# Loading two chunks of k ahead of the filter and moving four tap units into the wait for it, in a long-convolution (H3) layer with an MLP

## The chip, the cores and the metric

The kernel runs on one core of a Trainium2 chip. The metric is the device time of one execution in microseconds (us). Engines are named as the profile names them: PE is TensorE's matmuls, PEld its weight loads, DVE is VectorE, ACT is ScalarE, POOL is GpSimd, SP is SyncE, which issues the loads of k, v and ssm_k.

## The reference, cut to what matters

```python
k_shift = sum over t of k_pad[:, t:t+S, :] * shift_k[:, 3-t]     # 4 taps along the sequence
kv   = k_shift * v
kv_f = rfft2(kv padded to 2S);  kf_f = rfft2(ssm_k padded to 2S)
y    = irfft2(kv_f * kf_f)[:S] + kv * ssm_D
h    = x + layernorm(x) * y                                     # x = q
out  = h + relu(layernorm(h) @ w1) @ w2                         # the MLP, later in the kernel
```

S is 2048 and D is 512, in bfloat16. Two sequences are transformed: the filter ssm_k, and kv, the product of the shifted k with v. The change touches only the way there: loads, taps, the product with v, and the first stage of the filter's transform.

## The kernel before: the parts concerned

A *tap unit* is four matmuls that shift and scale one piece of k (128 channels by 512 tokens) into one PSUM buffer; there are 16 units, and units 4c to 4c+3 need chunk c of k and of v. After each unit VectorE multiplies the PSUM buffer with v into `kvx`. A *group* is the first stage of the filter's transform for an eighth of its columns: 64 pairs of a weight load and a small matmul. All PSUM tiles here come from one pool of eight buffers. In the code, letters such as `"DDDDADDA"` name the engine that copies out of PSUM: A is ScalarE, D is VectorE. A load *lands* when its last byte is in place.

```python
psum = pl.push("psF", bufs=8, space=PSUM)
...
# order of the loads on one queue; k and v are transposed by the DMA
for c, src in ((0, "k"), (0, "s"), (0, "v"), (1, "k"), (1, "v"), (2, "k"), (2, "v"), (3, "k"), (3, "v")):
    ...
table(cs, tsn)                    # sine table: two ScalarE operations
...
table(cc, r2[:], (0,))            # first half of the cosine table
...
def taps(u):
    c, rg = divmod(u, DC)
    ps = psum.tile([P, CH], F32, tag="ps", name="pkv")
    for j in range(KS):
        nc.tensor.matmul(out=ps[:], lhsT=wdiag[:, rg, j, :],
                         rhs=kT[:, rg, CH * c + 16 - j:CH * c + CH + 16 - j], ...)
    return u, ps

def times_v(u, ps):               # VectorE: kvx <- ps * v
    ...
first = [taps(u) for u in range(4)]
for q in range(8):                # 8 batches of 8 transposes of ssm_k, each copied out of PSUM
    to_rows(lambda n: skv[:, :, :, n], q, kfl, "DDDDADDA"[q])
    if q == 1:
        for u, ps in first:
            times_v(u, ps)
table(cc, r2[:], (1,))            # second half of the cosine table
...
for gb in range(8):
    for u in ((4, 5), (6,), (7, 8), (9,), (10, 11), (12,), (13, 14), (15,))[gb]:
        times_v(*taps(u))
    group_k(gb)                   # 64 pairs on TensorE, then four copies by ScalarE or VectorE
...
for q in range(8):                # 64 transposes of kvx: the yardstick "kvx start" below
    to_rows(lambda n: kvc[:, n // 4, :, n % 4], q, xfl, "DDADDADD"[q])
```

## Time and profile before

| | |
|---|---|
| median of 3 runs | 221.08 us (220.58 to 221.51) |
| span of the profiled run, granted clock | 218.7 us, 0.990 |
| transposes of ssm_k | 12.29 to 18.76 us |
| transposes of kvx begin ("kvx start") | 36.98 us |
| from kvx start to the end | 181.76 us |

The waits of the kernel before between 10 and 42 us (engine, line and tile, what it waited for, then us in all, times, longest) are:

```profile
PE pst L217 <- DMA pre<-in_A_ssm_k_dram: 2.1, 1, 2.1
PE ps L244 <- issue: 1.4, 2, 0.7
...
DVE kvx L278 <- DMA vT<-in_A_v_dram: 1.7, 2, 1.0
```

The first line is the wait that the change wants to fill. The second counts time in which TensorE waited for nothing that the profile shows.

### The profile page before, as it was taken

To read this page: it belongs to the slowest core of one execution; us is meant where nothing else is said; L and a number is where in the kernel's file an instruction comes from. 1 tells how busy PE (TensorE), PEld (TensorE's weight loads), DVE (VectorE), ACT (ScalarE), POOL (GpSimd) and SP (SyncE) were. 2 spreads that over 40 slices of the span, in tenths; PEclk is the share of its full clock that TensorE was granted. 3 is DMA by queue.
4 is the path that set the end of the run, shared out by engine and by line. 5 is a ranking of instruction groups with operands and counts; after the bars stand their busy time and mean duration, and the time that the engine had idled before them with its cause. 6 is when DMAs were issued, how large, how long until landed. Compare 5 with 4: busy or idle time off the path is not lost.

```text
span 218.7 us, 7281 instructions
## 1 busy us (share of the span) xinstructions
PE 202.8 (93%) x3103; PEld 139.4 (64%) x3122; DVE 148.2 (68%) x304; ACT 127.7 (58%) x242; POOL 65.9 (30%) x99
## 2 busy tenths in 40 slices
PE   7879889999979999989987899999999999999993
PEld 2276446999968999879965587444444444444442
DVE  7978868899979999957968779742973257130032
ACT  2587858788867888858966699003740066206500
POOL 6059920000029999969200120210021002000000
PEclk9969999999999999999999999999999999999999
DMA  6999960000000000059970000332022110421012
GB/s 96 383 224 191 142 136 7 3 4 3 6 3 0 1 0 3 1 134 216 305 252 3 6 0 3 42 77 55 24 52 63 42 47 0 96 57 42 0 42 54
DMA packets 30383, 15.40 MB, mean 70 GB/s; under 512 B 25520, under 2 KB 29072, under 8 KB 30224
## 3 DMA queue, kind: packets, MB, share of 16 engines
q1 hardware_dynamic: 29520, 14.76, 29.9%
q8 instruction: 24, 0.39, 0.8%
q10 hardware_dynamic: 832, 0.20, 0.4%
q14 instruction: 7, 0.06, 0.1%
HBM read 7.08 MB, written 2.10 MB: 42 GB/s over the span
## 4 chain that ended last, share of the span: by engine, by line
PE 83%; ACT 6%; DMA 4%; issue 2%; DVE 2%; SPq 1%; ACTq 0%
PE ps2m L568 17%; PE ps1m L556 16%; PE pz L482 8%; PE psi L449 7%; PE psy L375 7%; PE pst L217 5%; PE ps L244 4%; PE pkv L271 4%; PE ps2k L259 4%; DMA pre<-in_A_ssm_k_dram 4%; PE ps2k L261 3%; PE u L259 3%; PE u L261 3%; ACT ecore L143 1%; SPq L121 1%
## 5 line engine op out<-in xcount | busy, mean ns | idle before, releaser
L556 PE MATMUL ps1m<-hlnT,w 128*128 128x512 bf16 (+3 forms) x219 | 39.5, 336 | 0.3
L558 ACT ACTIVATE h1T<-ps1m 128x512 bf16<-128x512 f32 (+3 forms) x55 | 27.4, 514 | 21.2 <-PE ps1m L556 20.3
L568 PE MATMUL ps2m<-w,h1T 128*128 128x512 bf16 (+3 forms) x177 | 38.9, 366 | 0.7 <-issue 0.3
L570 DVE TENSOR_TENSOR o<-ps2m,xh 128x512 bf16<-128x512 f32 (+1 forms) x17 | 11.1, 659 | 38.1 <-PE ps2m L568 37.6
L556 PEld LDWEIGHTS <-w 128*128 128x128 bf16 (+1 forms) x220 | 21.7, 100 | 17.6 <-issue 1.4
L568 PEld LDWEIGHTS <-h1T 128*128 128x128 bf16 (+1 forms) x187 | 17.6, 98 | 21.2 <-issue 3.1
L365 DVE TENSOR_TENSOR t<-u,kf 128x704 fp32r<-128x704 f32 x32 | 26.7, 887 | 2.9 <-ACT usb L361 2.6
L365 POOL TENSOR_TENSOR t<-usb,kf 128x320 fp32r<-128x320 f32 x32 | 28.1, 922 | 1.4 <-ACT usb L361 1.0
L493 ACT CAST zt<-pz 128x512 bf16<-128x512 f32 x16 | 8.4, 592 | 29.2 <-PE pz L482 29.2
L482 PE MATMUL pz<-bp,ecore 32*32 32x128 f32 x1024 | 22.5, 384 | 2.3 <-issue 1.4
L231 ACT CAST a<-ps 128x512 fp32r<-128x512 f32 (+1 forms) x42 | 21.2, 575 | 4.3 <-PE ps L244 4.2
L502 POOL TENSOR_SCALAR rstd<-mv 128x4 f32<-128x4 f32 (+1 forms) x7 | 1.6, 232 | 70.3 <-DVE mv L509 70.3
L482 PEld LDWEIGHTS pz<-bp,ecore 32*32 32x32 f32 x1024 | 14.2, 103 | 9.4 <-issue 5.4
L231 ACT CAST kf<-psy 128x512 fp32r<-128x512 f32 x30 | 17.4, 640 | 1.7 <-PE psy L375 0.2
L233 DVE CAST a<-ps 128x512 fp32r<-128x512 f32 (+1 forms) x26 | 16.1, 647 | 3.1 <-PE ps L244 2.9
L507 DVE BATCH_NORM_STATS2 st<-xh 128x6 f32<-128x512 bf16 x28 | 17.4, 680 | 0.0
L449 PE MATMUL psi<-dre,kf 128*128 128x256 f32 x64 | 15.5, 284 | 0.9 <-ACT kf L231 0.9
L375 PE MATMUL psy<-t,ipos 128*128 128x512 f32 x48 | 15.8, 391 | 0.0
L271 PE MATMUL pkv<-kT,wdiag 128*128 128x512 bf16 x56 | 14.8, 380 | 0.8 <-DMA kT<-in_A_k_dram 0.3
L449 PE MATMUL psi<-dim,kf 128*128 128x256 f32 x64 | 15.4, 283 | 0.0
L209 POOL TENSOR_SCALAR c2n<-c2s 128x512 fp32r<-128x512 f32 x8 | 11.9, 1559 | 8.9 <-ACT c2s L177 8.9
L449 PEld LDWEIGHTS psi<-dre,kf 128*128 128x128 f32 x64 | 12.3, 192 | 1.3 <-ACT kf L231 1.3
(115 smaller groups left out, 377.0 us busy)
## 6 DMA issues: line engine op xcount, KB each, us to landing
pre<-in_A_ssm_k_dram SPq DMA_DIRECT2D x1, 2048.0 KB, 8.7
out_dram<-o SPq DMA_DIRECT2D x58, 32.0 KB, 1.6
xh<-in_A_q_dram SPq DMA_DIRECT2D x4, 384.0 KB, 6.8
w<-in_B_w_dram SPq DMA_DIRECT2D x1, 1376.0 KB, 12.7
w<-in_B_w_dram SPq DMA_DIRECT2D x1, 1280.0 KB, 15.8
xh<-in_A_q_dram SPq DMA_DIRECT2D x4, 128.0 KB, 2.8
hlnT<-hln SPq DMA_TRANSPOSE x12, 2.4
w<-in_B_w_dram SPq DMA_DIRECT2D x1, 96.0 KB, 15.4
```

The lines of the kernel that those rows point to most:

```text
L231: nc.scalar.copy(out=o, in_=i)
L233: nc.vector.tensor_copy(out=o, in_=i)
L259: nc.tensor.matmul(out=ps[:, kk, :], lhsT=w_re[:, k1, :], rhs=a_in(col(k1, 0)), start=True, stop=False, skip_group_check=True)
L271: nc.tensor.matmul(out=ps[:], lhsT=wdiag[:, rg, j, :], rhs=kT[:, rg, CH * c + 16 - j:CH * c + CH + 16 - j], start=(j == 0), stop=(j == KS ...
L365: eng.tensor_tensor(out=t[:, :, j, :], in0=in0.unsqueeze(1).to_broadcast([P, 2, n, 2]), in1=kfr[:, :, j, ks], op=ALU.mult)
L375: nc.tensor.matmul(out=psy[:], lhsT=m_[:], rhs=t_.rearrange("p j k -> p (j k)"), start=first, stop=not first)
L449: nc.tensor.matmul(out=ps[:, i, :], lhsT=kf[:, c, 4 * m:4 * m + 4, :].rearrange("p r k -> p (r k)"), rhs=d[:].rearrange("p a b -> p (a b)" ...
L482: nc.tensor.matmul(out=pz[32 * a:32 * a + 32, r4, l4, :], lhsT=ecore[rows, rho, n2, :], rhs=rhs, start=(rho == 0), stop=(rho == 1), tile_p ...
L507: nc.vector.bn_stats(out=st[:, t % 4, :], in_=xh[:, t, :])
L556: nc.tensor.matmul(out=ps1[:fsz, :], lhsT=w1[:, c, fc * P:fc * P + fsz], rhs=hlnTs[sc][:, c, part], start=(c == 0), stop=(c == DC - 1))
L558: nc.scalar.activation(out=h1s[sc][:fsz, fc, part], in_=ps1[:fsz, :], func=ACT.Relu)
L568: nc.tensor.matmul(out=ps2[:], lhsT=h1s[sc][:ksz, fc, i * P:(i + 1) * P], rhs=w2[:ksz, fc, ds], start=(fc == 0), stop=(fc == NFC - 1))
```

## The change

The intent is to give TensorE work while ssm_k is on its way. The second chunk of k is loaded ahead of ssm_k, so that eight tap units instead of four run before its transposes. Units 0 to 3 are copied out of PSUM by ScalarE and multiplied with v later on GpSimd, which reads that copy. Both halves of the cosine table come early, the groups get a new order of units, and the new letters give VectorE 12 of the groups' 32 copies instead of 8.

```diff
-    for c, src in ((0, "k"), (0, "s"), (0, "v"), (1, "k"), (1, "v"), (2, "k"), (2, "v"), (3, "k"), (3, "v")):
+    for c, src in ((0, "k"), (1, "k"), (0, "s"), (1, "v"), (0, "v"), (2, "k"), (2, "v"), (3, "k"), (3, "v")):
...
+    first = [taps(u) for u in range(8)]
+    ck = early.tile([P, DC, CH], F32, name="ck")
+    for u, ps in first[0:4]:
+        nc.scalar.copy(out=ck[:, u, :], in_=ps)
...
-    table(cc, r2[:], (0,))
+    table(cc, r2)
...
+        if h == 1:
+            for u in range(4):
+                times_v(u, ck[:, u, :], nc.gpsimd)
...
-        stage1(gb, kfl, ..., "AADAAADA")
+        stage1(gb, kfl, ..., "ADAADADA")
-    first = [taps(u) for u in range(4)]
...
-        to_rows(lambda n: skv[:, :, :, n], q, kfl, "DDDDADDA"[q])
+        to_rows(lambda n: skv[:, :, :, n], q, kfl, "DDDDDDAA"[q])
         if q == 1:
-            for u, ps in first:
+            for u, ps in first[4:8]:
                 times_v(u, ps)
-    table(cc, r2[:], (1,))
...
-        for u in ((4, 5), (6,), (7, 8), (9,), (10, 11), (12,), (13, 14), (15,))[gb]:
+        for u in ((8, 9), (10,), (11,), (), (12,), (13,), (14,), (15,))[gb]:
```

More of the change, by code (lines that the diff above doesn't have):

```diff
@@ L95 @@
     nc.sync.dma_start(out=wsh[:], in_=A_shift_k.rearrange("(r p) j -> p r j", p=P))
-    pre = slotA.tile([P, 4096 + 2048], I32, tag="A", name="pre")
+    pre = slotA.tile([P, 4096 + 2 * 2048], I32, tag="A", name="pre")
     skf = pre[:, 0:4096].bitcast(BF16)
@@ L159 @@
     nc.gpsimd.iota(r3[:], pattern=[[1, 64]], base=0, channel_multiplier=0)
-    r2 = early.tile([P, 32, 64], I32, name="w_r")
-    nc.gpsimd.iota(r2[:], pattern=[[2, 32], [128, 64]], base=1, channel_multiplier=0)
+    r2 = pre[:, 6144:8192].rearrange("p (k n) -> p k n", n=64)
+    nc.gpsimd.iota(r2, pattern=[[2, 32], [128, 64]], base=1, channel_multiplier=0)
     n1c = early.tile([P, 1], F32, name="n1c")
@@ L178, in table, with taps, times_v @@
                                  scale=hsc[:, dp:dp + 1], bias=hbi[:, dp:dp + 1])
+    kvx = early.tile([P, 16, DC, 32, 4], BF16, name="kvx")
+    def taps(u):
+        c, rg = divmod(u, DC)
+        ps = psum.tile([P, CH], F32, tag="ps", name="pkv")
+        for j in range(KS):
+            nc.tensor.matmul(out=ps[:], lhsT=wdiag[:, rg, j, :], rhs=kT[:, rg, CH * c + 16 - j:CH * c + CH + 16 - j],
+                             start=(j == 0), stop=(j == KS - 1))
+        return u, ps[:]
+    def times_v(u, ps, eng=nc.vector):
+        c, rg = divmod(u, DC)
+        split = "p (a h l) -> p a h l"
+        eng.tensor_tensor(out=kvx[:, :, rg, 8 * c:8 * c + 8, :].rearrange("p h a l -> p a h l"),
+                                in0=ps.rearrange(split, h=16, l=4),
+                                in1=vTs[c][:, rg, :].rearrange(split, h=16, l=4), op=ALU.mult)
     t1 = early.tile([P, 64], I32, name="f1_t")
@@ L192 @@
     _sin(dsc[:], t3[:], 64)
+    first = [taps(u) for u in range(8)]
+    ck = early.tile([P, DC, CH], F32, name="ck")
+    for u, ps in first[0:4]:
+        nc.scalar.copy(out=ck[:, u, :], in_=ps)
     tsn = pre[:, 4096:6144].rearrange("p (k n) -> p k n", n=64)
-    _turns(nc, tsn, r2[:], n2c[:], 8192, False)
+    _turns(nc, tsn, r2, n2c[:], 8192, False)
     table(cs, tsn)
@@ L201 @@
     nc.vector.tensor_copy(out=f1lo[:], in_=f1d[:])
-    _turns(nc, r2[:], r2[:], n2c[:], 8192, True)
-    table(cc, r2[:], (0,))
+    _turns(nc, r2, r2, n2c[:], 8192, True)
+    table(cc, r2)
     dtab = consts.tile([P, 8, DC, 8], BF16, name="dtab")
@@ L209 @@
         nc.gpsimd.tensor_single_scalar(out=cn[:, hs, :], in_=cs[:, hs, :].bitcast(F32), scalar=-1.0, op=ALU.mult)
-        if h == 0:
+        if h == 1:
+            for u in range(4):
+                times_v(u, ck[:, u, :], nc.gpsimd)
+        if h == 7:
             nc.gpsimd.tensor_copy(out=dtab[:], in_=d0[:].rearrange("p r (o g) -> p o r g", g=8))
@@ L262, in stage2 @@
                              skip_group_check=True)
-    kvx = early.tile([P, 16, DC, 32, 4], BF16, name="kvx")
-    def taps(u):
-        c, rg = divmod(u, DC)
-        ps = psum.tile([P, CH], F32, tag="ps", name="pkv")
-        for j in range(KS):
-            nc.tensor.matmul(out=ps[:], lhsT=wdiag[:, rg, j, :], rhs=kT[:, rg, CH * c + 16 - j:CH * c + CH + 16 - j],
-                             start=(j == 0), stop=(j == KS - 1))
-        return u, ps
-    def times_v(u, ps):
-        c, rg = divmod(u, DC)
-        split = "p (a h l) -> p a h l"
-        nc.vector.tensor_tensor(out=kvx[:, :, rg, 8 * c:8 * c + 8, :].rearrange("p h a l -> p a h l"),
-                                in0=ps[:].rearrange(split, h=16, l=4),
-                                in1=vTs[c][:, rg, :].rearrange(split, h=16, l=4), op=ALU.mult)
     def group_k(gb):
-        stage1(gb, kfl, lambda o, j, n: a1k[:, :, 32 * o + j:32 * o + j + n], "AADAAADA")
-    first = [taps(u) for u in range(4)]
+        stage1(gb, kfl, lambda o, j, n: a1k[:, :, 32 * o + j:32 * o + j + n], "ADAADADA")
     kfl = early.tile([P, 32, 2, 64, 2], BF16, name="kfl")
```

## The prediction

> **What bounds the kernel now.** I read the page first, then the chain that ended last in order of time, then busy time by stages, then the timelines of DVE, ACT, POOL and the DMA queue. The page's engine shares of the chain:
>
> ```profile
> PE 83%; ACT 6%; DMA 4%; issue 2%; DVE 2%; SPq 1%; ACTq 0%
> ```
>
> TensorE carries the end almost throughout. The change touches only the work before about 41 us; the rest should shift as a block. The early chain:
>
> ```profile
> 3.56 8.69 DMA pre<-in_A_ssm_k_dram
> ...
> 12.29 6.47 PE pst L217 x64
> 18.76 0.22 PE pkv L271
> ...
> 19.87 1.99 ACT c2c L177
> ...
> 26.91 0.62 issue
> ...
> 31.63 0.73 issue
> ...
> 36.98 3.77 PE pst L217 x64
> ```
>
> The reader is to see that the kernel waits for ssm_k until 12.25, transposes it for 6.47 us, is held by a sine table on ACT near 20 us, and reaches the second set of transposes (those of kvx) at 36.98. That last start is my yardstick. The same 64 transposes take 3.77 us there; the tile view of pst shows why:
>
> ```profile
> L217 PE MATMUL pst<-ident,pre x64: 219/298/311, 12.3 to 18.5; 128*128 128x128 bf16 x64
> L217 PE MATMUL pst<-ident,kvx x64: 219/219/248, 37.0 to 40.5; 128*128 128x128 bf16 x64
> ```
>
> Busy time by stage (columns PE, PEld, DVE, ACT, POOL, granted clock, DMA share, GB/s) confirms it: PE is idle from 10.20 to 12.29, then runs at a clock of 0.74.
>
> ```profile
> 12.30:18.76 6.46, 6.46 (x65) 6.39 (x66) 5.31 (x9) 4.20 (x4) 5.33 (x5) 0.74 1.31 231
> 20.40:36.98 16.58, 14.45 (x546) 8.07 (x553) 12.90 (x20) 12.31 (x23) 8.47 (x14) 1.00 0.72 119
> ```
>
> The second row is the stage that matters most: PE and DVE both near full. The DMA queue's issues and two DVE rows show what stands behind it:
>
> ```profile
> 1.25 2.24 SPq L121 DMA_TRANSPOSE kT<-in_A_k_dram  x1
> 3.56 0.57 SPq L118 DMA_DIRECT2D pre<-in_A_ssm_k_dram  x1
> 4.17 7.82 SPq L123 DMA_TRANSPOSE vT<-in_A_v_dram  x1
> 12.03 2.15 SPq L121 DMA_TRANSPOSE kT<-in_A_k_dram  x1
> ...
> 16.49 3.46 SPq L121 DMA_TRANSPOSE kT<-in_A_k_dram  x1
> ...
> 24.40 3.87 SPq L123 DMA_TRANSPOSE vT<-in_A_v_dram  x1
> ```
>
> ```profile
> 20.39 1.29 DVE L278 TENSOR_TENSOR kvx<-pkv,vT 128x512 bf16<-128x512 f32 x2 [0.77 <-DMA vT<-in_A_v_dram]
> ...
> 32.09 0.69 DVE L278 TENSOR_TENSOR kvx<-pkv,vT 128x512 bf16<-128x512 f32 x1 [0.97 <-DMA vT<-in_A_v_dram]
> ```
>
> One queue sends a transposed chunk every 2.2 us or so. By issue plus time to landing the third chunk of k is there at 22.5 (16.49 + 6.0) and the last of v at 32.0 (24.40 + 7.6). After that DVE needs 5.5 us to its last copy at 37.62. So the last v chunk, not PE alone, anchors this stage.
>
> [...] clock 0.50 from 13.07 to 16.48, one 3.41 us window[...].
> [...] The DMA view of short windows finds one such 0.02 MB fetch in each of 18 to 21, 24 to 28 and 28 to 30 us. The first two coincide with dead spells of the transposes (about 1.2 and 2 us), and PE's two "issue" gaps above follow the later two.
> [...]
> [...] the DVE product with v took 0.69 us both beside GpSimd's negations and after them.
>
> **The change part by part.**
>
> *Loads.* The second k chunk goes ahead of ssm_k. It costs one issue, 2.15 us, and 0.52 MB at some 240 GB/s, 2.2 us. So ssm_k lands near 14.4 instead of 12.25, and k's second chunk near 8.6 (3.5 + 5.0) instead of 17.0. Then v's second chunk lands near 16.7 and its first near 19.2. From the third k chunk on, the bytes ahead in the queue are as before: I expect it at 21.2 to 22.5 and the last v at 30 to 32.
>
> *TensorE.* Four units (16 matmuls at 0.216 us each, 3.5 us) move from the 20 to 37 us stage into the wait: PE is busy 6.58 to 13.65, and the gap before the transposes is under 1 us. They should then run at full clock, so 6.47 us of throttled time is no longer intrinsic. But transposes 4 to 7 reuse the PSUM buffers of units 4 to 7, which DVE frees only when v's second chunk is there: 16.7 + 4 x 0.62 = 19.2, then one batch of 8 x 0.059 = 0.5 gives 19.7. Before, they ended at 18.76. The sooner clock is mostly eaten here.
>
> *ScalarE.* Four copies of 0.52 us, the last after unit 3, end at about 11.0. Both sine tables follow without a break, 2 x 2.06 + 2 x 2.1 = 8.3, to 19.3; then the four half evacuations, 4 x 0.53, to 21.4. DVE's evacuations end at 19.2 + 4 x 0.62 = 21.7. So stage 1 could start at 21.7, against 20.42, but without the 1.99 us hold by the table.
>
> *New order on PE.* Units 8 and 9 stand ahead of the first stage-1 group. They need the third k chunk: 22.2 or so. PE then idles from 19.7 to 22.2, and group 0 begins at 22.2 + 2 x 0.87 = 23.9.
>
> *The stage after that.* PE has 8 units x 0.87 + 8 groups x 0.65 = 12.1 us, ending at 34.3. DVE has 8 products and 12 copies (it was 8 copies) x 0.69 = 13.8 us from 23.1, so 36.9 with no gap. ACT has 20 x 0.52 = 10.4. DVE becomes the bound. Walking the eight buffers by hand with these durations, DVE is ready for product 12 at 30.3. If v's last chunk is there by then, the last product ends at 35.9 and the kvx transposes start there, 1.1 us sooner than 36.98; DVE's last copy ends at 37.2, 0.4 sooner. If v lands at 32.0, ten DVE operations (6.9 us) stand behind it instead of eight (5.5): last product 37.6, last copy 38.9, a loss of 0.6 to 1.3.
>
> *GpSimd.* Two negations from 15.1 end at 18.1; four products after v's first chunk, at an estimated 1.4 us each (0.92 us for 320 elements, scaled to 512), end at 24.8; six negations of 1.48, dtab 0.4 and the dre/dim work 3.7 end at 37.8. The first user is after 41 us, so it is all hidden.
>
> Sum: about -0.7 us if v comes in time, +1.0 if not. I judge the instruction fetch to fall earlier in the v transfer than before and give the timely case 60%: 0.6 x (-0.7) + 0.4 x 1.0 = 0.0. Against this stands the schedule itself: the empty slot for group 3 and the new letters for who copies look measured rather than guessed, for which I take off 0.3 us.
>
> **Rivals.**
> 1. *The gap of 19.7 to 22.2 throttles PE.* [...] At half speed unit 9, group 0 and unit 10 slip by some 1.6 us, DVE reaches product 12 at 31.9 and its last copy at 38.8: about 222.2. [...] I give it a little under one half; it overlaps with a late v.
> 2. *The transfers shorten.* If no fetch stalls the transposes, k's third chunk lands at 21.2 and v's last at 28 to 29. The DVE bound then starts a microsecond sooner: some 219.3. For it: the two dead spells sum to 3.2 us. Against: PE crosses the same fetch boundaries in the same period.
> 3. *GpSimd becomes the bound.* If its products took over 2.3 us each, the dre/dim work would run past 41.5 and hold the first write of kf, whose memory overlays the early tables. Against: 0.92 us for 320 elements in this trace. It would give 222 to 225; I give it 5%.
> 4. *The full intent:* 3.5 us of taps and 2 us of table hold both gained, some 216. The v anchor speaks against it.
>
> **Range and chances.** The three runs of before lie between 220.58 and 221.51, so 0.5 us either way is noise. The centre is 221.08 - 0.3 = 220.8. Rival 1 and rival 3's lower end set the upper end at 222.6, rival 2 with its luck the lower at 218.8. Two per cent is 4.4 us: 216.7 needs the full intent, 225.5 needs GpSimd to fail badly. Chances: faster 0.05, same 0.92, slower 0.03.
>
> **What would show it.** In the changed profile: ssm_k landing near 14.4; its transposes at 219 ns but with gaps from batch 4 on, where they wait for DVE; PE idle before units 8 and 9, ended by k's DMA; DVE over 0.85 busy from 23 us on; a DVE wait for v before product 12; GpSimd done before 40 us. The start of the kvx transposes against 36.98 should account for the whole difference in time. I am wrong if ssm_k lands before 13.5 or after 15.5, if the last v lands before 29, or if the spectrum stage waits for GpSimd.

Its sum stands with all its terms: 0.6 x (-0.7) + 0.4 x 1.0 = 0.0, less 0.3, gives the centre of 220.8. Rival 1: its chance and its 222.2 stand as the author's estimates. A "fetch" in it is a 16 KiB transfer on the instruction queue (five of them within the first 40 us of the kernel before).

## The result

The changed kernel took 223.56 us (223.36 to 223.69, 3 runs) against 221.08. The ratio is 1.0112 with a 95% interval of 1.0076 to 1.0149. A ratio here is the mean time of one kernel's fast runs over that of the other's from the same rounds, so not quite the ratio of the medians quoted beside it. The kernel is slower by about one per cent, inside the 2% band, and 0.96 us above the upper end of the predicted range.

The shares of the chain in the page of the changed kernel show where: less of it is TensorE and more is the DMA queue.

```profile
PE 79%; SPq 7%; ACT 3%; DVE 3%; DMA 3%; issue 3%; ACTq 0%
```

The early part of its chain of waits (start, us, what carried the end):

```profile
6.69 8.46 SPq L123
...
16.96 6.29 DMA kT<-in_A_k_dram
...
23.73 1.46 PE pkv L187 x6
25.20 0.72 PE ps L270 x64
25.91 0.61 DVE kvx L194
...
29.98 1.40 issue
...
39.90 3.70 PE pst L243 x64
```

The kvx transposes start at 39.90, 2.92 us later than before. From there to the end it is 221.76 - 39.90 = 181.86 us, against 181.76: everything happens before that line. The chain now runs through the queue to k's third chunk (16.96 + 6.29 = 23.25), then to two tap units and a group that starts only at 25.20, and later through a gap of 1.40 us that is put down to nothing but "issue".

The tile view of the two sets of transposes, and the busy time by stage (PE, PEld, DVE, ACT, POOL, granted clock, DMA share, GB/s):

```profile
L243 PE MATMUL pst<-ident,pre x64: 239/254/302, 15.5 to 21.2; 128*128 128x128 bf16 x64
L243 PE MATMUL pst<-ident,kvx x64: 218/219/219, 39.9 to 43.4; 128*128 128x128 bf16 x64
```

```profile
15.46:21.43 5.97, 5.96 (x64) 5.83 (x64) 4.95 (x8) 3.95 (x4) 3.90 (x4) 1.00 1.52 233
21.43:39.90 18.47, 14.12 (x538) 7.81 (x546) 12.57 (x21) 10.85 (x21) 15.32 (x20) 0.91 0.44 88
...
32.26:35.67 3.41, 3.19 (x69) 1.31 (x68) 2.18 (x4) 2.24 (x5) 3.35 (x9) 0.51 0.03 7
```

The transposes of ssm_k now run at full clock, 1.00, and still take 5.97 us, or 93 ns each, where those of kvx take 58. And the stage behind the transposes lasts 18.47 us, against 36.98 - 18.76 = 18.22 before, although four tap units, 3.5 us of TensorE's work, have left it. The last row lies in a stretch in which the granted clock was half (0.50 from 32.33 to 35.74); such a *half-clock window* lasted 3.41 us each time in the traces of the two kernels (13.11 to 16.52 before; 32.33 to 35.74 and 124.49 to 127.90 after).

The waits of the changed kernel in the same window, and three rows of VectorE's timeline (start, us, engine, operation, in brackets the idle time before and what ended it):

```profile
PE pst L243 <- DMA pre<-in_A_ssm_k_dram: 2.0, 1, 2.0
PE pkv L187 <- DMA kT<-in_A_k_dram: 1.9, 1, 1.9
PE ps L270 <- issue: 1.4, 1, 1.4
```

```profile
25.24 1.29 DVE L194 TENSOR_TENSOR kvx<-pkv,vT 128x512 bf16<-128x512 f32 x2 [2.53 <-PE pkv L187]
...
31.83 1.29 DVE L259 CAST a<-ps 128x512 fp32r<-128x512 f32 x2 [1.72 <-PE ps L270]
...
35.85 0.69 DVE L194 TENSOR_TENSOR kvx<-pkv,vT 128x512 bf16<-128x512 f32 x1 [1.11 <-PE pkv L187]
```

The wait for ssm_k has not shrunk in this run (2.0 against 2.1): the load that fills it also makes it later. (In the later r1 and r2, on one chip, it was 2.1 before and 1.1 after.) A second wait stands behind it, for k's third chunk. VectorE starts on product 8 at 25.24; unit 8 had ended about a microsecond earlier, so the releaser named is not the real one: the third chunk of v landed at 25.14. The last chunk of v landed at 29.77, and no wait for it is left. VectorE is idle three times where the prediction had it full.

### The profile page after: what moved, and what is told of

It reads as the page before. It is cut to its first block, busy times and chain, and to the rows that moved or that the text cites. A ratio compares the mean times of both kernels' runs of the same rounds, so it can differ in the third digit from the quotient of the medians.

```text
span 221.8 us, 7287 instructions
## 1 busy us (share of the span) xinstructions
PE 203.8 (92%) x3104; PEld 139.8 (63%) x3122; DVE 146.8 (66%) x304; ACT 128.2 (58%) x242; POOL 70.4 (32%) x103
## 4 chain that ended last, share of the span: by engine, by line
PE 79%; SPq 7%; ACT 3%; DVE 3%; DMA 3%; issue 3%; ACTq 0%
PE ps2m L574 17%; PE ps1m L562 16%; PE pz L488 10%; PE psi L455 7%; PE psy L381 6%; SPq L123 5%; PE ps L270 4%; PE ps2k L285 4%; PE ps2k L287 3%; PE u L285 3%; PE u L287 3%; PE pkv L187 3%; DMA kT<-in_A_k_dram 3%; SPq L121 2%; PE pst L243 2%
## 5 line engine op out<-in xcount | busy, mean ns | idle before, releaser
L564 ACT ACTIVATE h1T<-ps1m 128x512 bf16<-128x512 f32 (+3 forms) x55 | 27.4, 514 | 21.2 <-PE ps1m L562 20.3
L574 PEld LDWEIGHTS <-h1T 128*128 128x128 bf16 (+1 forms) x187 | 17.6, 98 | 21.2 <-issue 3.1
L257 ACT CAST a<-ps 128x512 fp32r<-128x512 f32 (+1 forms) x38 | 19.3, 568 | 7.9 <-PE ps L270 4.6
L259 DVE CAST a<-ps 128x512 fp32r<-128x512 f32 (+1 forms) x30 | 18.4, 649 | 4.1 <-PE ps L270 4.1
L488 PEld LDWEIGHTS pz<-bp,ecore 32*32 32x32 f32 x1024 | 14.4, 106 | 9.4 <-issue 5.6
L187 PE MATMUL pkv<-kT,wdiag 128*128 128x512 bf16 x57 | 15.8, 399 | 3.1 <-DMA kT<-in_A_k_dram 2.5
L455 PE MATMUL psi<-dre,kf 128*128 128x256 f32 x64 | 15.5, 284 | 0.9 <-ACT kf L257 0.9
L232 POOL TENSOR_SCALAR c2n<-c2s 128x512 fp32r<-128x512 f32 x8 | 11.8, 1506 | 10.2 <-ACT c2s L177 10.2
L455 PEld LDWEIGHTS psi<-dre,kf 128*128 128x128 f32 x64 | 12.3, 192 | 1.3 <-ACT kf L257 1.3
```

Of the source, the lines that this page charges most:

```text
L187: nc.tensor.matmul(out=ps[:], lhsT=wdiag[:, rg, j, :], rhs=kT[:, rg, CH * c + 16 - j:CH * c + CH + 16 - j], start=(j == 0), stop=(j == KS ...
L257: nc.scalar.copy(out=o, in_=i)
L259: nc.vector.tensor_copy(out=o, in_=i)
L455: nc.tensor.matmul(out=ps[:, i, :], lhsT=kf[:, c, 4 * m:4 * m + 4, :].rearrange("p r k -> p (r k)"), rhs=d[:].rearrange("p a b -> p (a b)" ...
L488: nc.tensor.matmul(out=pz[32 * a:32 * a + 32, r4, l4, :], lhsT=ecore[rows, rho, n2, :], rhs=rhs, start=(rho == 0), stop=(rho == 1), tile_p ...
L564: nc.scalar.activation(out=h1s[sc][:fsz, fc, part], in_=ps1[:fsz, :], func=ACT.Relu)
```

## The experiments

Eighteen runs were made, of thirteen new kernels and, again, the two known ones; all gave a correct result. "ssm_k" is the start of its transposes, "kvx start" that of the kvx transposes, "issue" the sum of TensorE's unexplained waits ahead of the groups' matmuls between 10 and 42 us (single waits of 0.2 us ahead of a tap unit are left out), all in the one profiled run; the ratio is to the kernel before in the same rounds.

| run | median us | before us | ratio (95%) | ssm_k | kvx start | issue |
|---|---|---|---|---|---|---|
| before | 221.08 | | | 12.3 | 36.98 | 1.4 |
| after | 223.56 | 221.08 | 1.0112 (1.0076 to 1.0149) | 15.5 | 39.90 | 1.4 |
| e1 | 221.98 | 221.35 | 1.0047 (0.9959 to 1.0135) | 14.3 | 38.36 | 0.9 |
| e2 | 220.47 | 221.35 | 0.9993 (0.9906 to 1.0080) | 13.6 | 38.02 | 0.5 |
| e3 | 220.93 | 221.35 | 1.0003 (0.9924 to 1.0082) | 14.6 | 38.31 | 1.0 |
| e4 | 221.20 | 221.35 | 1.0017 (0.9927 to 1.0108) | 14.0 | 38.36 | 1.2 |
| r1 | 220.57 | 220.51 | 0.9998 (0.9952 to 1.0044) | 12.5 | 36.60 | 0.8 |
| r2 | 222.05 | 220.51 | 1.0070 (1.0020 to 1.0119) | 14.6 | 38.17 | 0.9 |
| r3 | 220.29 | 220.51 | 0.9983 (0.9942 to 1.0024) | 14.2 | 36.76 | 2.0 |
| b1 | 220.08 | 220.51 | 0.9974 (0.9932 to 1.0015) | 9.7 | 36.48 | 0.5 |
| e5 | 221.84 | 220.03 | 1.0064 (1.0022 to 1.0105) | 14.3 | 37.84 | 1.8 |
| e6 | 220.14 | 220.03 | 0.9985 (0.9939 to 1.0031) | 14.7 | 35.67 | 0 |
| e7 | 222.65 | 220.03 | 1.0104 (1.0058 to 1.0151) | 16.5 | 40.46 | 0.4 |
| b2 | 221.22 | 220.03 | 1.0039 (0.9996 to 1.0083) | 15.2 | 36.79 | 0.2 |
| e8 | 222.62 | 220.67 | 1.0073 (1.0029 to 1.0117) | unusable | unusable | |
| b3 | 220.47 | 220.67 | 0.9972 (0.9919 to 1.0026) | 14.4 | 36.15 | 1.7 |
| e9 | 219.54 | 221.25 | 0.9940 (0.9881 to 1.0000) | 14.3 | 36.21 | 1.1 |
| e8b | 222.39 | 221.25 | 1.0061 (1.0015 to 1.0106) | 14.3 | 39.34 | 1.5 |
| e9b | 220.94 | 221.48 | 0.9960 (0.9905 to 1.0015) | 14.3 | 37.00 | 0.6 |
| e10 | 222.27 | 221.48 | 0.9956 (0.9884 to 1.0028) | 14.6 | 38.03 | 2.9 |

A profiled run is one draw: of one kernel two traces have kvx start over a microsecond apart (39.90 and 38.17 for the changed kernel, 38.31 and 36.76 for e3 and r3); the landing of ssm_k and the place of the half-clock windows differ between them too (in the changed kernel 15.41 and 14.55, and 32.33 and 22.37). e7's profiled run was slow, and e10's median counts three slow runs that its ratio leaves out.

### One part of the change at a time (three rounds)

**e1** puts the second k chunk ahead of ssm_k in the kernel before, and nothing else.

```diff
-    ... ((0, "k"), (0, "s"), (0, "v"), (1, "k"), (1, "v"), ...
+    ... ((0, "k"), (1, "k"), (0, "s"), (0, "v"), (1, "v"), ...
```

> The kernel before with one thing changed: the second chunk of k is loaded ahead of ssm_k. Theory L (the later ssm_k is the loss): ssm_k lands near 15.4 us instead of 12.25, the kvx transposes start 2 to 3 us later than 36.98, and the time is 223 to 224. Rival V (the stage is anchored by the last loads of k and v, whose place in the queue does not change): the kvx transposes move by less than 1 us and the time is 221 to 222.

**e2** is the change without its loads: ssm_k second again, four lead units, the units' old order among the groups; the copies on ScalarE, the products on GpSimd and the early table stay.

```diff
-    ... ((0, "k"), (1, "k"), (0, "s"), (1, "v"), (0, "v"), ...
+    ... ((0, "k"), (0, "s"), (1, "k"), (1, "v"), (0, "v"), ...
-    first = [taps(u) for u in range(8)]
+    first = [taps(u) for u in range(4)]
...
-        if q == 1:
-            for u, ps in first[4:8]:
-                times_v(u, ps)
...
-        for u in ((8, 9), (10,), (11,), (), (12,), (13,), (14,), (15,))[gb]:
+        for u in ((4, 5), (6,), (7, 8), (9,), (10, 11), (12,), (13, 14), (15,))[gb]:
```

> The changed kernel with ssm_k behind only one chunk of k again, and four tap units leading instead of eight; ScalarE copies, GpSimd products, early table and the letters for who copies stay. Theory L: 220 to 221, near the kernel before or better. Rival O (the order of units and the gaps of TensorE after 21 us are the loss, not the load): also gone here, 220 to 221. Rival D (the 12 copies on VectorE instead of 8 are the loss): VectorE has 24 operations of 0.69 us after 19.5, so 222 to 223.

**e3** is the change with units 8 and 9 behind group 0.

```diff
-        for u in ((8, 9), (10,), (11,), (), (12,), (13,), (14,), (15,))[gb]:
+        for u in ((), (8, 9), (10,), (11,), (12,), (13,), (14,), (15,))[gb]:
```

> The changed kernel with units 8 and 9 moved behind the first stage-1 group, so that TensorE need not wait for the third chunk of k before it. Theory L: group 0 starts 3 us sooner, but what follows waits for the same chunk; the time falls by at most 1 us, 222.5 to 223.5. Rival O (that wait of 1.87 us is the loss): 221 to 222.

**e4** makes both halves of the cosine table early in the kernel before.

```diff
-    table(cc, r2[:], (0,))
+    table(cc, r2[:])
...
-    table(cc, r2[:], (1,))
```

> The kernel before with one thing changed: both halves of the cosine table made before the transposes of ssm_k. If the 1.99 us hold by the table near 20 us was worth its length, 219 to 220; if ScalarE's share of the transposes' evacuation only waits in its place, 220.5 to 222.

Measured: 1.0047, 0.9993, 1.0003 and 1.0017, each with an interval of 0.8 to 0.9% to either side, because the kernel before itself ranged from 218.54 to 222.11 in these rounds. None is decided by its time. Two readings hold all the same. Of the four, e1 leans most towards slower. And e4, which takes away the table's hold of 1.99 us (0.9%) and little else, gained nothing that can be seen, and its interval, from 0.9927, leaves no room for the whole 0.9%: the hold was a step of the chain, but not worth its length. Three rounds were too few for effects of half a per cent; the rest ran with five.

### The kernels again with five rounds

**r1** is the kernel before, **r2** the changed one, **r3** is e3, without an edit, on one chip.

> The kernel before, unchanged, for its profile on the same chip as the next two and for the size of the noise: ratio 1.000 within 0.005. The first four experiments showed ssm_k landing between 13.6 and 14.6 us whatever the order of loads, while the first profile had 12.25; this run tells whether the chip or the kernel makes that difference.

> The changed kernel, unchanged, beside the kernel before. If the first result holds on another chip: 223 to 224 and a ratio near 1.011. If it hung on where the clock window or the instruction fetches fell in that first job: 220.5 to 222.

> The changed kernel with units 8 and 9 behind group 0, as in the third experiment, now beside the changed kernel itself on one chip. Theory O (the wait for the third chunk of k, put ahead of group 0, and what follows from it is the loss): 1.5 to 3 us faster than the changed kernel. Theory L (the later ssm_k): within 1 us of it.

The kernel before against itself gives 0.9998. The changed kernel is slower again, though by less than at first, 1.0070, and r3 is not, 0.9983: a difference of 222.05 - 220.29 = 1.76 us for nothing but the place of two tap units. kvx starts at 36.60, 38.17 and 36.76. So the loss of the change lies in that order, and the parts around it come out even. ssm_k landed at 12.46 in r1 and 14.55 in r2, so the load ahead cost 2.1 us on this chip. It did not on the chip of the first four runs: there ssm_k landed at 13.52 (e2) and 13.95 (e4) as the second load, and at 14.29 (e1) and 14.60 (e3) as the third, 0.3 to 1.1 us apart. Each of these figures is one trace.

The waits of r2, TensorE's and VectorE's, show two candidates:

```profile
PE pkv L187 <- DMA kT<-in_A_k_dram: 1.6, 1, 1.6
...
DVE kvx L194 <- DMA vT<-in_A_v_dram: 2.4, 1, 2.4
```

TensorE waits for k's third chunk (landed 22.04) before unit 8. VectorE, whose operations lie in the trace in the order of the program, waits for v's third chunk (landed 24.03) before product 8 (24.12), and group 0's copies stand behind it (the first at 26.34). In r2 a half-clock window from 22.37 to 25.78 follows the first wait. In it units 8 and 9 took 3.36 us for the two, instead of 1.74, and the window is a third candidate.

### Which of the two waits

**e5** loads k's third chunk one place sooner in the changed kernel.

```diff
-    ... (0, "s"), (1, "v"), (0, "v"), (2, "k"), (2, "v"), ...
+    ... (0, "s"), (1, "v"), (2, "k"), (0, "v"), (2, "v"), ...
```

> The changed kernel with one thing changed: the third chunk of k is loaded ahead of the first chunk of v, which only GpSimd uses. The order of TensorE's work stays as in the change. Theory O (the wait of 1.6 to 1.9 us for the third chunk ahead of group 0 is the excess loss): no wait ahead of unit 8, and about the time of the run with units 8 and 9 later, ratio to the kernel before 0.995 to 1.001. If the order of units as such, not the wait for the load, is the loss: ratio 1.005 to 1.011 as the changed kernel.

Measured: 1.0064, as slow as the changed kernel. TensorE's wait for k is gone, and the loss is not. The waits of e5:

```profile
PE ps L270 <- DVE kvx L194: 2.1, 3, 1.3
...
DVE kvx L194 <- DMA vT<-in_A_v_dram: 2.7, 1, 2.7
```

VectorE now waits 2.7 us for v's third chunk, and TensorE 2.1 us for VectorE to free a buffer. The clock was 1.00 through the whole stage, so this order is slow without any half-clock window; what is left of the candidates is VectorE's wait.

**e8** and **e8b** are one kernel: the changed one, with TensorE's program untouched, but VectorE's products of units 8 and 9 behind group 0's copies.

```diff
     for gb in range(8):
         for u in ((8, 9), (10,), (11,), (), (12,), (13,), (14,), (15,))[gb]:
-            times_v(*taps(u))
+            if gb:
+                times_v(*taps(u))
+            else:
+                first.append(taps(u))
         group_k(gb)
+        if gb == 0:
+            for u, ps in first[8:]:
+                times_v(u, ps)
```

> TensorE's program is that of the changed kernel, units 8 and 9 ahead of group 0; only VectorE's products of units 8 and 9 with v stand behind group 0's copies in its queue. Two waits are told apart. If what the new order costs is VectorE's queue, held by a product that waits for the third chunk of v (landing near 24 us), group 0's copies no longer wait, and the run lies beside the one with units 8 and 9 moved altogether: ratio 0.998 to 1.002, kvx transposes near 36.8 us. If it is TensorE's own wait for the third chunk of k, it lies beside the changed kernel: ratio 1.004 to 1.008, kvx near 38. If the fetch of instructions gives all gains back, the difference between the two is under 0.5 us either way.

> The same kernel as the run with the products of units 8 and 9 later, whose profiled run was disturbed (1053 us) and left no trace to read. Expected by the theory of two waits one behind the other: TensorE waits 1.5 to 2.5 us for the third chunk of k after ssm_k's transposes, VectorE no longer waits for v ahead of group 0's copies, kvx transposes at 37.7 to 38.5 us, ratio 1.004 to 1.009. If the first run's ratio was an accident of a disturbed chip: 0.998 to 1.002.

The profiled run of e8 took 1053 us and was of no use as a trace (in it TensorE's transposes took 747 ns each, the median, against 254 and 219 in the changed kernel, and VectorE's copies 692); one run of the kernel before took 658 us in the same rounds. The timed runs were normal: 1.0073, and 1.0061 when repeated. In e8b's waits VectorE no longer waits for v, and TensorE's wait for k is back:

```profile
PE pkv L187 <- DMA kT<-in_A_k_dram: 1.6, 1, 1.6
```

kvx starts at 39.34 there, later than expected; a half-clock window from 30.89 to 34.30 is in it (there a unit took 1.82 us and a group 0.97, instead of 0.97 and 0.62).

**e9** and **e9b** join the two edits, so that neither wait is left while units 8 and 9 still stand ahead of group 0. **e10** joins e5's load order with e3's order of units.

> Two runs took away one wait each and stayed slow: the third chunk of k sooner (1.0064; VectorE then waited 2.7 us for v's third chunk ahead of group 0's copies), and the products of units 8 and 9 later (1.0073, no usable trace; TensorE's wait for the third chunk of k was left in). This one takes both away, with units 8 and 9 still ahead of group 0 on TensorE. If the two waits stand one behind the other, and either alone keeps the loss: no TensorE wait above 0.5 us for kT, none above 0.7 for kvx, kvx transposes at 36.5 to 37.2 us, ratio 0.996 to 1.001. If the order of units on TensorE is dear for another reason: ratio 1.004 to 1.008.

> The kernel with both waits taken away, again and on another pass, since its interval (0.988 to 1.000) only just excludes no gain and it is the candidate that beats both kernels. Expected, if it is a real gain: ratio 0.991 to 0.999, kvx transposes at 36.0 to 36.9 us. If the first run was luck: 0.999 or above.

> The changed kernel with the third chunk of k sooner and with units 8 and 9 behind group 0, so that neither wait can occur and the order on TensorE is the other one. If the order itself costs nothing once nothing waits, and the fetch of instructions sets the pace of both: within 0.3% of the run with both waits taken away on the same chip, kvx transposes at 36.0 to 36.9 us, issue gaps of 1 to 2 us in sum. If the order of units matters by itself: over 0.5% apart.

Measured: 0.9940, 0.9960 and 0.9956. Each edit alone left the kernel 0.6 to 0.7% slower than before; both together leave it faster than that by 222.39 - 219.54 = 2.85 us in the medians of e8b and e9, which ran on the same chip. (For e9 that is better than the 0.996 to 1.001 expected.) In e9's waits little is left:

```profile
PE ps L270 <- issue: 1.1, 2, 0.7
...
DVE kvx L194 <- DMA vT<-in_A_v_dram: 0.5, 1, 0.5
```

So the theory holds that the two waits stand one behind the other: take one away and the other takes its place. e10, with the other order on TensorE and also without the waits, lies within 0.04% of e9b on the same chip, though on three fast runs of six. The order as such costs nothing that intervals of 0.6 to 0.7% to either side could show; the waits that it runs into do. (e9b's and e10's kvx starts missed what was expected: e9b had a half-clock window from 28.97 to 32.38, with a unit of 1.68 us and a group of 0.97, and e10 an issue gap of 1.93 us.)

One thing these runs do not separate. A half-clock window takes about 0.008 from a run's mean clock (an estimate, 3.41 x 0.5 of some 220 us). All 20 undisturbed runs of the kernels in which TensorE waits for k ahead of unit 8 (the first result, r2, e8 and e8b) have a mean clock of 0.977 to 0.992, while five of r3's six, four of e5's six and seven of the twelve of e9 and e9b have 0.998 or more. Within e9 the three runs at 0.992 took 1.6 us longer on average than the three at 1.00; within e9b no such order shows. So e5, at 1.00, shows what VectorE's wait costs by itself, but in e8 and e8b the cost of TensorE's wait may be in part that of the half clock, and no run here tells them apart.

### What the "issue" gaps are

In every kernel with the full groups the gaps ahead of the groups' matmuls lie at the same places of TensorE's program, though not each place has one in each run. Counted in order, they precede the weight loads number 352, 480 and 608: 128 pairs of a weight load and a matmul apart, 256 instructions. In r3's timeline of TensorE (the bracket holds the gap):

```profile
28.77 0.18 PE L270 MATMUL ps<-f_hi,kfl 32*128 32x64 bf16 x1 [1.06 <-issue]
...
32.50 0.18 PE L270 MATMUL ps<-f_hi,kfl 32*128 32x64 bf16 x1 [0.47 <-issue]
...
36.23 0.18 PE L270 MATMUL ps<-f_hi,kfl 32*128 32x64 bf16 x1 [0.46 <-issue]
```

They are 3.73 us apart, twice. In the traces of the kernels before and after, each of the two gaps at these places ends 1.2 to 1.4 us after a 16 KiB transfer on the instruction queue has ended (before: 27.53 after 26.18, 32.35 after 30.97; after: 31.39 after 30.19, 39.38 after 38.13). Such a transfer is called a fetch here, and every place 128 pairs apart from these, with a gap or without one, a boundary. With no load under way a fetch began 0.6 to 1.2 us after TensorE crossed a boundary (before: 32.35 to 33.50 and 36.26 to 36.85; after: 31.39 to 32.51 and 35.94 to 36.77); in r3, whose view gives the start to within 0.35 us, 0.8 to 1.4 us. With transposing loads under way it was 1.6 and 2.4 us in the kernel before (22.78 to 24.40, 27.53 to 29.90) and 2.0 in the changed one (27.00 to 29.00), but in e9 only about 1 and in r2 0.6 to 0.8 us, so no rule is shown. In the kernel before, the DMA engines stood nearly idle from 25.2 to 26.9 us (busy share 0.04), beside and after the fetch from 24.40 to 26.18. The fetch itself takes 0.9 to 1.8 us in these two traces. In r2 the boundaries are at 27.39, 30.74, 34.20 and 37.65, 3.35 to 3.46 us apart, with a gap at each of the last three. The shortest block without a gap at its end took 3.22 us (b2).

How much work is in a block? At full clock a group of 64 pairs takes 0.61 us and a tap unit of 4 pairs 0.87 us. Before, the stage holds 8 groups and 12 units, 560 pairs or 4.38 blocks, and 8 x 0.61 + 12 x 0.87 = 15.3 us of work: 3.5 us for a block. After, with 8 units, it is 544 pairs or 4.25 blocks and 11.8 us: 2.8 us for a block. As an estimate from these numbers, TensorE before worked just about as fast as its instructions came; after, it would outrun them by 0.6 to 0.9 us a block (against 3.35 and 3.73). By this estimate it was the four units taken out, few and long instructions (16 matmuls of 0.216 us), that hid the fetch.

**e6** tests it by r3 with half the small matmuls of each k group (the low half of a split table is dropped, so this is less exact arithmetic, within the tolerance) and two idle matmuls of 512 columns per group in their place. **e7** keeps all the small matmuls and adds the same two.

```diff
-        stage1(gb, kfl, ..., "ADAADADA")
+        stage1(gb, kfl, ..., "ADAADADA", fs=((f1hi, True, True),), extra=2)   # e6
+        stage1(gb, kfl, ..., "ADAADADA", extra=2)                             # e7
...
+            for _ in range(extra):
+                nc.tensor.matmul(out=<first ps of the group>, lhsT=wz[:, 0:P], rhs=wz[:], start=True, stop=True)
```

> The variant with units 8 and 9 later, but in each of the eight k groups the 32 pairs of weight load and matmul for the low half of the table are left out (a less exact result, on purpose) and two matmuls of 128x512 on constants are put in (0.43 us): TensorE's matmul time per group rises from about 0.61 to 0.73 us, its instructions fall from 128 to 68. Theory F (from group 2 on TensorE waits for its own instructions, 16 KiB blocks of 256, which arrive no faster than one in about 3.5 us): the issue gaps of 2.0 us in all go, the kvx transposes start 1 us or more sooner than 36.8, ratio 0.988 to 0.996. Rival P (the stage is bound by TensorE's matmul time): ratio 1.001 to 1.005.

> The control of the run with half the instructions: the same two extra matmuls of 128x512 per k group, 3.4 us in all, but the low half kept. Theory F: the extra time falls partly into the gaps in which TensorE waits for instructions, so the kvx transposes start 1 to 2 us later than without it, ratio 1.003 to 1.008. Rival P (bound by matmul time): 3 to 3.5 us later, ratio 1.012 to 1.015. A slack in which all of it fits: ratio 0.998.

In e6 the gaps are gone, 0 against 2.0 us in r3, and these are all of TensorE's waits in the window:

```profile
PE ps L273 <- ACT kfl L252: 1.2, 1, 1.2
PE pst L243 <- DMA pre<-in_A_ssm_k_dram: 1.0, 1, 1.0
```

Its stage, from the end of ssm_k's transposes to kvx start, is about 15.0 us long against r3's 16.5, though TensorE had no less to do: the two added matmuls take 0.43 us, the 32 dropped pairs some 0.3. In e7, with as many instructions but more time for each block, one gap of 0.4 us is left (the profiled run was slow, but in this stage its groups took 0.61 to 0.68 us, as at full clock):

```profile
PE ps L273 <- issue: 0.4, 1, 0.4
```

So in these runs the gaps go with the number of instructions, set against the time that they take: 2.0 us in r3, none with half the small matmuls (e6), 0.4 with more time for as many (e7). What the fetch costs in the end isn't settled by times, and both times missed what the theory of the fetch expected. e6 came out at 0.9985 (0.988 to 0.996 was expected) and r3 at 0.9983, in different passes. e7's 1.0104 lies between what the fetch (up to 1.008) and what TensorE's matmul time (from 1.012) would have given. Its 16 matmuls of 0.216 us are 3.5 us of work, and it was slower than r3 by about 1.2% or 2.7 us, which leaves up to about 0.8 us absorbed by the gaps.

### Searching for a better kernel

**b1** turns the intent round: in the kernel before, ssm_k is loaded first of all, and the taps follow its transposes.

```diff
-    ... ((0, "k"), (0, "s"), (0, "v"), (1, "k"), ...
+    ... ((0, "s"), (0, "k"), (0, "v"), (1, "k"), ...
-    table(cc, r2[:], (0,))
+    table(cc, r2[:])
...
-    first = [taps(u) for u in range(4)]        # ahead of the transposes
...
-        to_rows(lambda n: skv[:, :, :, n], q, kfl, "DDDDADDA"[q])
...
+        to_rows(lambda n: skv[:, :, :, n], q, kfl, "D")
+    first = [taps(u) for u in range(4)]        # behind the transposes, as are the products with v
...
-        for u in ((4, 5), (6,), (7, 8), (9,), (10, 11), (12,), (13, 14), (15,))[gb]:
+        for u in ((4,), (5, 6), (7,), (8, 9), (10,), (11, 12), (13,), (14, 15))[gb]:
```

> The kernel before with ssm_k ahead of every chunk of k, all eight evacuations of its transposes on VectorE, both table halves early, and the tap units behind the transposes. Theory S (what the early stage waits for is ssm_k, and the taps can follow k as it comes): ssm_k lands near 8.5, its transposes end near 14, the kvx transposes start at 33 to 35 and the time is 217 to 219. Rival V (the last chunk of v anchors the stage): v lands near 29 to 31 as before, then four products stand behind it, the kvx transposes start at 36 to 37 and the time is 220.5 to 221.5.

The tile view of b1 shows that the transposes began 2.6 us sooner than before, and the end of the stage came hardly sooner:

```profile
L217 PE MATMUL pst<-ident,pre x64: 231/261/352, 9.7 to 15.8; 128*128 128x128 bf16 x64
L217 PE MATMUL pst<-ident,kvx x64: 219/219/247, 36.5 to 40.0; 128*128 128x128 bf16 x64
```

TensorE then had all 16 units and 8 groups still to do, 16 x 0.87 + 8 x 0.61 = 18.8 us of the 20.4 that it took. The ratio is 0.9974, unclear. So the hoped-for start at 33 to 35 did not come; the last v landed at 30.07, but what filled the stage was TensorE's own work.

**b2** frees ScalarE sooner: r3 with e5's load order, the second half of the cosine table moved behind group 3, and other letters for who empties the ssm_k batches (the table's input gets a tile of its own, so that it lives long enough). **b3** is b2 with that half in four pieces behind groups 2 to 5.

```diff
-        to_rows(lambda n: skv[:, :, :, n], q, kfl, "DDDDDDAA"[q])
+        to_rows(lambda n: skv[:, :, :, n], q, kfl, "DDADADAD"[q])
...
+        if gb == 3:                                # b2
+            table(cc, r2, (1,))
...
+        if gb in (2, 3, 4, 5):                     # b3
+            k8 = slice(8 * (gb - 2), 8 * (gb - 2) + 8)
+            table(cc[:, k8, :], r2[:, k8, :], (1,))
```

> A try at a better kernel: the changed kernel with units 8 and 9 behind group 0, the third k chunk ahead of v's first, the second half of the cosine table made after group 3, and two of the eight evacuations on ScalarE in the middle instead of at the end. Group 0 should start near 20.7 instead of 21.6 us; by theory F the stage then still needs some 15 us for its 544 pairs of instructions, so the kvx transposes start near 35.7 and the ratio to the kernel before is 0.993 to 0.998.

> The run with ScalarE free sooner, whose second cosine half held ScalarE from 30.2 to 32.2 us and TensorE for 1.0 us with it, now with that half in four pieces of about 0.55 us after groups 2 to 5. If the hold was the loss: no TensorE wait above 0.5 us for ScalarE, kvx transposes near 35.8 us, ratio 0.992 to 0.999. If instruction fetch is the bound in any case: the hold is replaced by issue gaps, kvx at 36.5 or later, ratio 0.998 to 1.003.

b2 missed what was expected of it (0.993 to 0.998, kvx near 35.7). In it TensorE waits for a copy that the table holds up on ScalarE; in b3 that wait is gone and the fetch has taken its place. One line of each kernel's waits:

```profile
PE ps L271 <- ACT a L258: 1.0, 1, 1.0
```

```profile
PE ps L271 <- issue: 1.7, 3, 0.7
```

b3's boundaries are 4.19, 3.73 and 3.73 us apart. The ratio, 0.9972, is what was expected if the hold was the loss, the gaps are what was expected of the fetch, and kvx start at 36.15 lies between the two. No kernel is shown to beat both. e9 comes nearest, with 0.9940 and 0.9960: about half a per cent, where one interval ends at 1.0000 and the other at 1.0015.

## Why the prediction was wrong, point by point

- **The loads: right in size on one chip, and more scattered than allowed for.** ssm_k landing later by 2.15 us was measured as 2.1 from r1 to r2, and as 0.3 to 1.1 among e1 to e4. In the first profile it was 15.41, a microsecond beyond the 14.4; eleven later traces with ssm_k third in the queue had it between 14.2 and 14.6, one at 15.1 and one at 16.4. So about a microsecond of the miss is the draw of the first run or of its chip: on another one the same kernel took 222.05 (r2), inside the predicted range. That is luck too; the step named below failed in both.
- **The transposes of ssm_k: wrong.** "so 6.47 us of throttled time is no longer intrinsic" was a false reading. That a shorter gap ahead of them would bring the full clock was inference from one trace. The clock was 1.00, and at that they took 5.97 us; a batch of eight costs 0.75, not 0.5. The half clock had cost only about half a microsecond before, 6.47 against 5.97. No wait for PSUM buffers from batch 4 on was seen either: the one wait of the transposes is that for ssm_k, 2.0 us. They ended at 20.5 in r2, against 19.7, so this term missed by 0.8.
- **The third chunk of k: right.** TensorE idle until 22.2, ended by k's DMA, was 22.04 in r2 and 23.25 in the first profile.
- **The step that failed is "The stage after that": VectorE with "13.8 us from 23.1, so 36.9 with no gap", and the last v chunk as its anchor.** The last v came in time, at 28.75 in r2 and 29.77 in the first profile, before the 30.3 that the walk asked for. That was the timely case, for which 35.9 was predicted as the end of the last product. It ended at 37.93 in r2 and 39.72 in the first profile. Three terms make the difference. Product 8 began at 24.12 and 25.24 instead of 23.1, because v's *third* chunk landed at 24.03 and 25.14; the walk placed only the last (+1.0 and +2.1). VectorE was idle for 2.15 and 3.1 us until that last product instead of never. And its 18 operations followed each other every 0.65 and 0.63 us instead of 0.69 (-0.8 and -1.1). The sums, +2.35 and +4.1, overshoot the misses of 2.0 and 3.8 by 0.3; the walk had put in 0.4 beyond 18 x 0.69.
- **What the idle time waited for** is TensorE, which had gaps in its instruction supply (0.9 us in r2, 1.4 in the first profile) and a half-clock window, 3.41 us long, in either. The prediction knew the fetch as a thing that delays v's transposes, not as the pace of TensorE itself. That 12.1 us of TensorE work could be done in 12.1 us was the same error as VectorE's: as an estimate, 4.25 blocks at 3.35 us (the shortest of r2's blocks that ended in a gap) are 14.2 us.
- **Rival 1, half clock after the wait for k,** happened word for word in r2 (22.37 to 25.78), and even its time, about 222.2, was met there (222.05). e5 had no such window and was as slow, so the loss does not need it; whether it is part of the loss where TensorE waits for k is open, as said above. In the first profile of the same kernel the window was ten microseconds later (32.33 to 35.74). Of **rival 2** (shorter transfers) r2 had the last v at 28.75, but not the third k at 21.2, nor the gain. **Rival 4** (the full intent) did not come; **rival 3** neither: GpSimd's products took 4.55 us for four, 1.14 each against the estimated 1.4, and it was done at 36.99, against the 37.8 predicted.
- **The 0.3 us taken off because the new order "looked measured" was wrong** in sign: the place of units 8 and 9 is worth 1.76 us against the change.
- **The noise of 0.5 us** was read off three runs. In later rounds the same kernel before, fast and slow runs together, lay between 218.54 and 224.18, one disturbed run of 657.97 left out.
- **Two small slips without effect:** 3.5 + 5.0 is 8.5 and not 8.6, and the window given as 13.07 to 16.48 is 13.11 to 16.52 by the profile's own zero.

Where the expected gain went is so answered in three parts. The load ahead of ssm_k gives back up to 2.1 us of it at once (on one chip; 0.3 to 1.1 on another). The order of units runs into two waits, one behind the other, and loses 1.8 more; that makes the change slower, and it is shown by r2 against r3 and by e5, e8b and e9, save that the half clock is not separated from TensorE's wait. What then remains, 3.5 us of taps fewer in the stage, is in part taken by the fetch: shown are the gaps and what removes them (e6), while their share in microseconds is an estimate. Why the transposes of ssm_k need 93 ns each was not tested: their source steps by 128 bytes within a partition, that of kvx by 8, but no run here changes only that.

## What to carry to other kernels

When two engines wait for two loads at the same place of the program, fixing either alone may show nothing (e5 1.0064, e8b 1.0061, both edits together 0.9940 in e9): look at which wait ends second before judging an edit, and test the pair. Before moving long instructions out of a stage of many short ones, look at the gaps that are put down to "issue" and count the instructions between them: here they lay 256 apart, and where TensorE was held at one after the other a block took 3.35 to 3.73 us (r2, r3). If the work in a block is less than that, the time that the long instructions took may have been free. And a load put ahead of another fills the wait only if it does not lengthen it by as much (here ssm_k came 2.1 us later from r1 to r2, against a wait of 2.1).
